# Fifth key block of the product with the values in two column tiles, and the 1e-9 of the softmax sums on ScalarE

## The chip, the cores and the metric

The kernel runs on one core of a Trainium2 chip. The metric is the device time of one execution in microseconds; of several runs the median is given. TensorE's granted clock is 2.4 GHz or 1.2 GHz, and the profile gives it as a share of the former.

## The reference

Attention with 2 batches, 8 heads, 576 positions and 64 channels per head, all in fp32, and behind it two MoE-like layers of 1152 tokens (512 to 2048 to 512 channels).

```python
scores = scale * np.matmul(q, k.transpose(0, 1, 3, 2))
...
scores = scores + bias.transpose(2, 0, 1)[None, :, :, :]
scores = scores - np.max(scores, axis=-1, keepdims=True)
attn = np.exp(scores)
attn = attn / (np.sum(attn, axis=-1, keepdims=True) + 1e-09)
return np.matmul(attn, v).astype(np.float32)
```

The bias comes from a small network over log-distances (hidden size 32); the two layers are `g(x @ w_in) @ w_out` with a rational function and a clipped square as g. The change touches the last three lines above: the 1e-9 and the product with v.

## The kernel before, in words

The queries are cut into blocks of 128 rows: a first one of 64 rows of both batches ("t") and four of 128 rows. A unit is a block with a pair of heads (`hp`), a pair is a unit with a batch: 4 pairs of the first kind and 32 full ones. For pair i and its heads e = 0 and 1 (tile t = 2i + e):

- `qk` (L322, TensorE): scores in PSUM, the two heads in two row tiles of the array;
- `ttr` (L337, VectorE): scores plus bias, with the row's minimum of the negated sum, into `P`;
- `exp` (L342, ScalarE): the exponential in place, with the row's sum into `m[:, 1, e]` (a second instruction reads the accumulator);
- `rec` (L346 and L347, VectorE, once for both heads): the sum plus 1e-9, and its reciprocal into `m[:, 2]`;
- `norm` (L146, mostly GpSimd): `P` times the reciprocal;
- `trans` (L367, TensorE) in three groups of three, each 128 by 128: of the 576 keys of both heads side by side nine blocks come out; block 4 holds the last 64 keys of head 0 and the first 64 of head 1 (whose keys run backwards);
- evacuation of each group to `PT` (L134, the helper `copy`, on ScalarE);
- `pv` (L380 and L383, TensorE): for block 4 one matmul of 128 columns with the values `Vt[hp][:, bb, 4]`, which hold zeros in the half of the rows that belongs to the other head; then for four blocks and both heads a matmul of 64 columns each into its half of the output's partitions;
- copies of the product (L400 ScalarE, L402 VectorE) into the inputs of the first layer, as a high and a low part.

All instructions of an engine run in the order in which they were written. A planner sets it: `at(step, engine, fn, pri, cost)` puts work into a step, `flex` leaves the engine to be chosen, and `run_step` goes through a step in order of `pri`, adds the costs to each engine's `load`, and for a `flex` takes the engine with the lowest load after its cost (`pick`); loads fall by a pace at each step. TensorE's work of a step comes behind the others', sorted likewise. For pair i the exponentials stand in steps 2i+2 and 2i+3, `rec` in 2i+4, the first group of transposes in 2i+6 and the others in 2i+7, their evacuations one step later, and `pv` in 2i+8. Between them lie the rows of the bias (L208, L206, L219, L142, L144) and the conversion of the layers' weights (L457 to L482).

`cst` is a tile of four columns of constants; three are in use (`setup2`), as bias operands of the layers' activations. Behind the attention the two layers run from a generator (`moe`, L652 and L695).

Of the kernel before, what the change touches and what calls it, by code (L numbers as in the profile page):

```python
# [8 lines left out]
AF = mybir.ActivationFunctionType  # L9
# [30 lines left out]
class Kernel:  # L40
# [21 lines left out]
    def setup2(self):  # L62
        nc, a, c = self.nc, self.a, self.const
        nc.gpsimd.memset(self.cst[:, 0:1], ADDC)
        nc.gpsimd.memset(self.cst[:, 1:2], 0.5)
        nc.gpsimd.memset(self.cst[:, 2:3], -0.5)

    def ab_consts(self):
        nc, c = self.nc, self.const
# [21 lines left out]
    def at(self, step, eng, fn, pri=0, cost=0.3):  # L91

        self.todo.setdefault(step, []).append((pri, eng, fn, cost))
# [191 lines left out]
    def attn(self, p, pq, ps, pss, x, cfg):  # L285
        nc, a, at = self.nc, self.a, self.at
        V, A, G, PE = nc.vector, nc.scalar, nc.gpsimd, nc.tensor
        halves = lambda z: z.rearrange("p (x c) -> p x c", x=2)
        K = [self.ring(f"K{h}").rearrange("p (b s) -> p b s", b=B) for h in range(H // 2)]
        Vt = [p.tile([128, B, 5, 128], F32, name=f"V{h}") for h in range(4)]  # L290
        self.K = K


        units = [(bk, hp) for bk in ("t", 0, 1, 2, 3) for hp in range(4)]
        pairs = []
        for n, (bk, hp) in enumerate(units):
            pairs += [(n, bk, hp, b) for b in ((0, 1) if bk != "t" else ("t",))]
        bias, Q, P, PT, sums, S_ = {}, {}, {}, {}, {}, {}
        vps = ps.tile([128, 2, 2, 128], F32, name="vps")
        first = {}  # L300
        for i, (n, *_) in enumerate(pairs):
            first.setdefault(n, 2 * i)

        def load_q(n):
            bk, hp = units[n]
            t = Q[n] = pq.tile([128, B, 128], F32, tag="Q", name="Q", bufs=4)
            if bk == "t":
                nc.sync.dma_start(t[:, :, 0:64], a["qt"][hp])
            else:
                nc.sync.dma_start(t, a["qm"][4 * bk + hp])  # L310

        def qk(i):

            n, bk, hp, b = pairs[i]
            for e in range(2):
                S_[2 * i + e] = pss.tile([128, 2, 512], F32, tag="s", name="sps", bufs=2)
            for x in range(2):
                for bb in (b,) if bk != "t" else range(2):
                    w, c = (128, 0) if bk != "t" else (64, 64 * bb)
                    for e in range(2):  # L320
                        r = slice(64 * e, 64 * e + 64)
                        PE.matmul(S_[2 * i + e][c:c + w, x, :288], lhsT=Q[n][r, bb, 0:w],  # L322
                                  rhs=f(K[hp])[r, bb, 288 * x:288 * x + 288], start=True, stop=True,
                                  tile_position=(64 * e, c))

        def tile_(t):
            i, e = divmod(t, 2)
            n, bk, hp, b = pairs[i]
            h = 2 * hp + e

            def ttr():
                if e == 0:
                    P[i] = p.tile([128, 2, S], F32, tag="P", name="P", bufs=cfg["pb"])
                    sums[i] = p.tile([128, 3, 2], F32, tag="m", name="m", bufs=6)
                o = P[i][:, 0] if e == 0 else P[i][:, 1][:, ::-1]
                bt = self.bias0[bk == 0][:, h] if bk in (0, "t") else bias[n, e][:]
                V.tensor_tensor_reduce(halves(o), S_.pop(t)[:, :, :288], halves(bt), -0.125, 3e38,  # L337
                                       ALU.add, ALU.min, sums[i][:, 0, e:e + 1])

            def exp():  # L340
                m, s = sums[i], P[i][:, e]
                A.activation(s, s, AF.Exp, bias=m[:, 0, e:e + 1], scale=-1.0, accum_out=m[:, 1, e:e + 1])  # L342

            def rec():
                m = sums[i]
                V.tensor_scalar(m[:, 2], m[:, 1], 1e-9, None, ALU.add)  # L346
                V.reciprocal(m[:, 2], m[:, 2])  # L347

            def norm(e_):
                s = P[i][:, e]  # L350
                self.copy(e_, s, s, sums[i][:, 2, e:e + 1])

            at(t + 1, "V", ttr, PAR["vp"][0], 0.69)
            at(t + 2, "A", exp, PAR["vp"][1], 0.77)
            if e:
                at(t + 2 + PAR["rec"], "V", rec, PAR["vp"][2])
            self.flex(2 * i + PAR['norm'] + PAR['norme'] * e, dict(G=PAR['cG'], V=PAR['cV'], A=PAR['cA']), norm, PAR['pe_'][0])

        def pair_(i):
            n, bk, hp, b = pairs[i]  # L360
            Pf = lambda: P[i].rearrange("p e c -> p (e c)")
            tp = {}

            def trans(c):
                t = tp[c] = ps.tile([128, 512], F32, tag="T", name="tps", bufs=3)
                for j in range(3):
                    PE.transpose(t[:, 128 * j:128 * j + 128], Pf()[:, 384 * c + 128 * j:384 * c + 128 * j + 128], self.ident)  # L367

            def evac(e, c):
                if c == 0:  # L370
                    PT[i] = p.tile([128, 9, 128], F32, tag="PT", name="PT", bufs=cfg["ptb"])
                dst = PT[i][:, 3 * c:3 * c + 3].rearrange("p a b -> p (a b)")
                self.copy(e, dst, tp.pop(c)[:, :384])

            def pv():
                o = vps[:, n % 2]
                for bb in ((b,) if b != "t" else (0, 1)):
                    c = slice(0, 128) if b != "t" else slice(64 * bb, 64 * bb + 64)
                    out = o[:, bb] if b != "t" else o[:, 0, c]
                    PE.matmul(out, lhsT=Vt[hp][:, bb, 4], rhs=PT[i][:, 4, c], start=True, stop=False)  # L380
                    for j in range(4):
                        for e in range(2):
                            PE.matmul(out[64 * e:64 * e + 64], lhsT=Vt[hp][:, bb, j, 64 * e:64 * e + 64],  # L383
                                      rhs=PT[i][:, (j, 5 + j)[e], c], start=False, stop=(j == 3))
                PT.pop(i), P.pop(i)

            for c in range(3):
                s = 2 * i + PAR['t0' if c == 0 else 't1']
                at(s, "P", lambda c=c: trans(c), PAR["pp"][2])
                self.flex(s + PAR['ev'], dict(A=PAR['eA'], V=PAR['eV']), lambda e, c=c: evac(e, c), PAR['pe_'][1])  # L390
            at(2 * i + PAR['pv'], "P", pv, PAR["pp"][3])
            if b != 0:
                o = {"t": [(0, 0, 128, 0)], 0: [(0, 0, 256, 128)], 1: [(1, 0, 256, 0)],
                     2: [(1, 0, 128, 256), (2, 128, 128, 0)], 3: [(2, 0, 256, 128)]}[bk]

                def out(k, u, c, w, d):
                    src = vps[:, n % 2].rearrange("p b q -> p (b q)")[:, c:c + w]
                    xh, xl = (x[k][u][:, hp, d:d + w] for k in range(2))
                    if k == 0:
                        A.activation(xh, src, AF.Copy)  # L400
                    else:
                        V.tensor_tensor(xl, src, f(xh), ALU.subtract)  # L402

                for y in o:
                    at(2 * i + PAR["xh"], "A", lambda y=y: out(0, *y), PAR["vp"][3])
                    at(2 * i + PAR["xl"], "V", lambda y=y: out(1, *y), PAR["vp"][4])

        def get_bias(n, e):
            bk, hp = units[n]
            h = 2 * hp + e  # L410
            bias[n, e] = self.load_bias(pq, bk, h, cfg["bias"])

        for t in range(2 * len(pairs)):
            tile_(t)
        for i in range(len(pairs)):
            at(2 * i, "P", lambda i=i: qk(i), PAR["pp"][0])
            pair_(i)
        for n in range(len(units)):
            at(first[n] - PAR["ql"], "end", lambda n=n: load_q(n), 1)
            for e in range(2) if n >= 8 else ():  # L420
                at(first[n] - cfg["ahead"] + e, "end", lambda n=n, e=e: get_bias(n, e), 2)
        for h in range(H):

            at(h, "G", lambda h=h: G.tensor_copy(self.bias0[0][64:128, h], self.bias0[0][0:64, h]), 0, 0.9)
            at(PAR['vl'][h], "end", lambda h=h: nc.sync.dma_start(Vt[h // 2][:, h % 2], a["v5"][h // 2, h % 2]), 3)

        return 2 * len(pairs) + 11
# [406 lines left out]
```

## Time and profile before

| what | value |
|---|---|
| time, median of 3 runs (lowest to highest) | 616.69 us (616.47 to 617.79) |
| profiled execution, span of its instructions | 615.9 us |
| difference of the two | 0.8 us |
| mean granted TensorE clock | 0.997 |
| busy: TensorE, VectorE, ScalarE, GpSimd | 95%, 78%, 66%, 57% |

The span runs from the first to the last instruction of one profiled execution; the time of a run holds what lies around it too. A busy share is that of the whole span, and the attention ends about a third into it, so what a change in the attention is worth is read from the windows and the chain of that part. The matmuls' ends are modelled and overlap: the starts tell more than the durations.

### The profile page before, as it was taken

The numbers are of one execution on the slowest core, as the hardware profiler recorded it, in microseconds if no ns is written. First come the engines' busy times: TensorE is split into PE (matmuls) and PEld (weight loads), VectorE is DVE, ScalarE is ACT, GpSimd is POOL, SyncE is SP. The second block draws the span as 40 slices with busy tenths as digits, with TensorE's granted clock in tenths as the row PEclk, the third lists the DMA queues.
The fourth block names the chain that finished last, engine by engine and source line by source line (L and its number), as shares of the span: only waits on it lengthen the run. The fifth ranks groups of instructions, "written<-read, shape, count | busy, mean of one in ns | idle before, by whom it ended". The sixth has DMA issues, their size and how long they took to land.

```text
span 615.9 us, 11246 instructions
## 1 busy us (share of the span) xinstructions
PE 584.2 (95%) x4084; PEld 519.1 (84%) x4084; DVE 479.0 (78%) x952; ACT 408.1 (66%) x878; POOL 348.7 (57%) x367
## 2 busy tenths in 40 slices
PE   5899998998999689999999999999999999999997
PEld 2356655566778589999999999999999999999997
DVE  6875777685679779889999888999996799594432
ACT  5976787776887799888878877644664554443330
POOL 0253334543557458679998886665674576384220
PEclk9999999999999999999999999999999999999999
DMA  6982256453644201232232221231323123020012
GB/s 207 252 273 80 83 180 205 139 185 104 190 154 150 92 24 46 69 102 70 69 103 69 70 69 51 88 102 69 103 103 103 57 85 99 1 70 1 24 42 89
DMA packets 25288, 62.71 MB, mean 102 GB/s; under 512 B 3601, under 2 KB 7569, under 8 KB 25233
## 3 DMA queue, kind: packets, MB, share of 16 engines
q1 hardware_dynamic: 25088, 61.90, 31.3%
q8 instruction: 32, 0.52, 0.4%
q14 instruction: 24, 0.19, 0.1%
q10 hardware_dynamic: 144, 0.10, 0.1%
HBM read 48.83 MB, written 9.62 MB: 95 GB/s over the span
## 4 chain that ended last, share of the span: by engine, by line
PE 79%; DVE 10%; ACT 5%; DMA 2%; issue 2%; POOL 1%; SPq 0%; DVEq 0%; POOLq 0%; ACTq 0%
PE outps L695 30%; PE inps L652 29%; PE sps L322 6%; PE vps L383 5%; PE bps L219 4%; PE tps L367 4%; PE vps L380 2%; DVE P L337 1%; DVE hid L208 1%; ACT PT L134 1%; DMA bias<-bd 1%; DVE wc L464 1%; ACT hid L206 1%; DVE wc L460 1%; DMA raw<-w 1%
## 5 line engine op out<-in xcount | busy, mean ns | idle before, releaser
L695 PE MATMUL outps<-gh,wo 128*128 128x384 f32 x768 | 209.7, 335 | 0.0
L558 POOL TENSOR_TENSOR gl<-v,gh 128x384 fp32r<-128x384 f32 x96 | 110.4, 1150 | 79.3 <-ACT gh L554 74.8
L695 PEld LDWEIGHTS outps<-gh,wo 128*128 128x128 f32 x768 | 139.9, 188 | 0.0
L695 PE MATMUL outps<-gl,wo 128*128 128x384 f32 x384 | 128.4, 334 | 0.0
L652 PE MATMUL inps<-x,wh 128*128 128x384 f32 x384 | 99.8, 341 | 5.5 <-DVE x L402 3.8
L146 POOL TENSOR_SCALAR P<-P,m 128x576 f32<-128x576 f32 x72 | 56.6, 792 | 68.8 <-DVE m L347 51.4
L337 DVE CUSTOM_DVE_ANT_0 P<-sps,bias 128x576 f32<-128x576 f32 x72 | 54.0, 750 | 35.4 <-PE sps L322 20.8
L652 PEld LDWEIGHTS inps<-x,wh 128*128 128x128 f32 x384 | 70.2, 190 | 6.7 <-DVE x L402 4.1
L695 PEld LDWEIGHTS outps<-gl,wo 128*128 128x128 f32 x384 | 72.1, 188 | 0.0
L521 ACT ACTIVATE v<-inps,cst 128x384 f32<-128x384 f32 x48 | 27.8, 580 | 66.7 <-PE inps L652 63.8
L652 PE MATMUL inps<-x2l,wh 128*128 128x384 f32 x192 | 64.7, 337 | 1.7 <-DVE x2l L628 1.7
L545 DVE SCALAR_TENSOR_TENSOR v<-v 128x384 f32<-128x384 f32 x48 | 39.5, 823 | 34.1 <-ACT v L521 33.9
L652 PE MATMUL inps<-x,wl 128*128 128x384 f32 x192 | 65.1, 339 | 0.0
L652 PE MATMUL inps<-x2h,wh 128*128 128x384 f32 x192 | 64.7, 337 | 0.0
L652 PE MATMUL inps<-x2h,wl 128*128 128x384 f32 x192 | 64.6, 336 | 0.0
L134 ACT ACTIVATE PT<-tps 128x384 f32<-128x384 f32 x108 | 48.6, 488 | 23.3 <-PE tps L367 23.0
L554 ACT ACTIVATE gh<-v 128x384 fp32r<-128x384 f32 x96 | 50.6, 527 | 20.1 <-DVE v L546 18.9
L525 POOL TENSOR_TENSOR q<-h,q 128x384 f32<-128x384 f32 x48 | 48.7, 1015 | 26.3 <-ACT q L518 25.8
L342 ACT ACTIVATE P<-P,m 128x576 f32<-128x576 f32 x72 | 55.9, 776 | 11.3 <-DVE m L337 11.3
L464 DVE SCALAR_TENSOR_TENSOR wc<-raw,wc 128x512 int32<-128x512 int32 x64 | 59.9, 946 | 0.0
L367 PEld LDWEIGHTS tps<-late,P 128*128 128x128 f32 x324 | 34.6, 141 | 20.8 <-issue 14.5
L219 PE MATMUL bps<-hid,w2s 128*32 128x288 f32 (+17 forms) x416 | 41.6, 472 | 8.4 <-DVE hid L208 7.0
(79 smaller groups left out, 1192.1 us busy)
## 6 DMA issues: line engine op xcount, KB each, us to landing
raw<-w SPq DMA_DIRECT2D x64, 512.0 KB
bd<-bbuf SPq DMA_DIRECT2D x24, 295.5 KB
bias<-bd SPq DMA_DIRECT2D x24, 288.0 KB
bias<-bbuf SPq DMA_DIRECT2D x12, 288.0 KB
V<-v SPq DMA_DIRECT2D x8, 320.0 KB
K<-kc SPq DMA_DIRECT2D x4, 576.0 KB
out<-acc SPq DMA_DIRECT2D x12, 192.0 KB
Q<-qm SPq DMA_DIRECT2D x16, 128.0 KB
```

The source lines that it names most:

```text
L134: nc.scalar.activation(out, x, AF.Copy, scale=scale)
L146: nc.gpsimd.tensor_scalar(out, x, scale, 1.0, ALU.mult, ALU.mult)
L219: nc.tensor.matmul(st[x][32 * j:32 * j + 32, :w], lhsT=w2, rhs=hid[j][:, x * w:x * w + w], start=True, stop=True, tile_position=(0, 32 * j))
L337: V.tensor_tensor_reduce(halves(o), S_.pop(t)[:, :, :288], halves(bt), -0.125, 3e38, ALU.add, ALU.min, sums[i][:, 0, e:e + 1])
L342: A.activation(s, s, AF.Exp, bias=m[:, 0, e:e + 1], scale=-1.0, accum_out=m[:, 1, e:e + 1])
L367: PE.transpose(t[:, 128 * j:128 * j + 128], Pf()[:, 384 * c + 128 * j:384 * c + 128 * j + 128], self.ident)
L464: return [(dict(V=0.7), lambda e: V.scalar_tensor_tensor(tc, words[:, :, 0], 29, tc, ALU.logical_shift_right, ALU.bitwise_or))]
L525: return [lambda: G.tensor_tensor(o["q"], o["h2"], o["q"], ALU.add)] if m == 0 else []
L554: return [lambda: A.activation(gh, o["v"], AF.Copy)]
L558: return [lambda: G.tensor_tensor(gl, o["v"], f(o["gh"]), ALU.subtract)]
L652: nc.tensor.matmul(ps[:, :U], lhsT=w[:, c], rhs=y[:, c], start=(t == 0), stop=(t == 11))
L695: nc.tensor.matmul(ps[:, :U], lhsT=w[:, c], rhs=y, start=(t == 0), stop=(t == 11))
```

## The change

The product with the fifth key block (block 4) is written as two matmuls of 64 columns, one for each head, into the two halves of the output's partitions, like the other four blocks; it stays first and now carries the start of the sum. The addition of 1e-9 leaves VectorE; an activation with identity on ScalarE, with the constant as bias operand, stands behind the second exponential of a pair (same step, next in `pri`) and has a planner's cost of 0.1. The constant takes the fourth column of `cst`.

```diff
         nc.gpsimd.memset(self.cst[:, 2:3], -0.5)
+        nc.gpsimd.memset(self.cst[:, 3:4], 1e-9)
...
+            def eps():
+                m = sums[i]
+                A.activation(m[:, 2], m[:, 1], AF.Identity, bias=self.cst[:, 3:4])
+
             def rec():
                 m = sums[i]
-                V.tensor_scalar(m[:, 2], m[:, 1], 1e-9, None, ALU.add)
                 V.reciprocal(m[:, 2], m[:, 2])
...
             if e:
+                at(t + 2, "A", eps, PAR["vp"][1] + 0.1, 0.1)
                 at(t + 2 + PAR["rec"], "V", rec, PAR["vp"][2])
...
-                    PE.matmul(out, lhsT=Vt[hp][:, bb, 4], rhs=PT[i][:, 4, c], start=True, stop=False)
-                    for j in range(4):
+                    for j in (4, 0, 1, 2, 3):
                         for e in range(2):
                             PE.matmul(out[64 * e:64 * e + 64], lhsT=Vt[hp][:, bb, j, 64 * e:64 * e + 64],
-                                      rhs=PT[i][:, (j, 5 + j)[e], c], start=False, stop=(j == 3))
+                                      rhs=PT[i][:, (j, 5 + j if j < 4 else 4)[e], c],
+                                      start=(j == 4), stop=(j == 3))
```

## Rows read from the trace of the kernel before

**Rows 1.** The page, busy us (share of the span) and instructions of each engine.
```profile
PE 584.2 (95%) x4084; PEld 519.1 (84%) x4084; DVE 479.0 (78%) x952; ACT 408.1 (66%) x878; POOL 348.7 (57%) x367
```

**Rows 2.** The page, chain that ended last, share of the span by line.
```profile
PE outps L695 30%; PE inps L652 29%; PE sps L322 6%; PE vps L383 5%; PE bps L219 4%; PE tps L367 4%; PE vps L380 2%; DVE P L337 1%; DVE hid L208 1%; ACT PT L134 1%; DMA bias<-bd 1%; DVE wc L464 1%; ACT hid L206 1%; DVE wc L460 1%; DMA raw<-w 1%
```

**Rows 3.** Windows: us, length, busy us of each engine, PEclk, DMA share, GB/s.
```profile
20.00:190.00 170.00, 157.69 (x1560) 104.05 (x1562) 121.94 (x355) 131.25 (x320) 77.69 (x113) 1.00 0.53 164
200.00:220.00 20.00, 14.40 (x83) 13.47 (x83) 14.02 (x26) 14.28 (x30) 7.76 (x8) 0.91 0.22 74
```

**Rows 4.** Waits, 0 to 213 us: waiter <- releaser, us in total, times, longest.
```profile
ACT PT L134 <- PE tps L367: 23.0, 25, 2.0
DVE P L337 <- PE sps L322: 20.8, 17, 2.6
...
PEld vps L380 <- ACT PT L134: 12.0, 21, 2.1
```

**Rows 5.** Timeline of TensorE, a product at 181 us: start, us, instructions.
```profile
180.27 1.20 PE L367 MATMUL tps<-late,P 128*128 128x128 f32 x9
181.40 0.49 PE L380 MATMUL vps<-PT,V 128*128 128x128 f32 x2
181.81 1.09 PE L383 MATMUL vps<-PT,V 128*64 128x128 f32 x16
182.84 0.51 PE L322 MATMUL sps<-K,Q 64*128 64x288 f32 x1
```

**Rows 6.** Timeline of TensorE, a product at 150 us.
```profile
149.86 0.39 PE L380 MATMUL vps<-PT,V 128*128 128x128 f32 x2
150.18 1.09 PE L383 MATMUL vps<-PT,V 128*64 128x128 f32 x16
151.21 0.51 PE L322 MATMUL sps<-K,Q 64*128 64x288 f32 x2
```

**Rows 7.** Timeline of TensorE, the product of the first pair.
```profile
37.82 0.33 PE L380 MATMUL vps<-PT,V 128*128 128x64 f32 x2
38.08 0.69 PE L383 MATMUL vps<-PT,V 128*64 128x64 f32 x16
38.70 0.44 PE L380 MATMUL vps<-PT,V 128*128 128x64 f32 x2
39.06 0.69 PE L383 MATMUL vps<-PT,V 128*64 128x64 f32 x16
39.68 0.52 PE L322 MATMUL sps<-K,Q 64*128 64x288 f32 x2
```

**Rows 8.** Groups by line and form, and line L82: busy us, mean ns; duration.
```profile
L134 ACT ACTIVATE PT<-tps 128x384 f32<-128x384 f32 x108 | 48.6, 488 | 23.3 <-PE tps L367 23.0
...
L383 PE MATMUL vps<-PT,V 128*64 128x128 f32 x512 | 35.0, 279 | 0.0
...
L383 PE MATMUL vps<-PT,V 128*64 128x64 f32 x128 | 5.5, 228 | 0.0
...
L521 ACT ACTIVATE v<-inps,cst 128x384 f32<-128x384 f32 x48 | 27.8, 580 | 66.7 <-PE inps L652 63.8 <-POOL wo L149 2.7
...
L346 DVE TENSOR_SCALAR m<-m 128x2 f32<-128x2 f32 x36 | 8.2, 227 | 0.0
...
L82 ACT ACTIVATE rt<-rt x1: 203/203/203, 95.0 to 95.0; 128x1 f32<-128x1 f32 x1
```

**Rows 9.** Chain that ended last in order of time: start, us, what.
```profile
190.35 0.51 DVE m L346
```

**Rows 10.** Timeline of ScalarE, 164 to 169 us.
```profile
164.01 0.19 ACT L342 ACTIVATION_READ_ACCUMULATOR P<-P,m 128x1 f32 x1
...
165.09 0.87 ACT L134 ACTIVATE PT<-tps 128x384 f32<-128x384 f32 x2
...
168.84 0.87 ACT L134 ACTIVATE PT<-tps 128x384 f32<-128x384 f32 x2 [0.98 <-PE tps L367]
```

**Rows 11.** Timeline of VectorE, the removed addition behind that exponential.
```profile
165.20 0.16 DVE L346 TENSOR_SCALAR m<-m 128x2 f32<-128x2 f32 x1
```

## The prediction

> **What bounds the kernel now.** I read the busy table first: TensorE is busy for 95% of the span and no other engine for over 78% [rows 1]. Of the chain that ended last TensorE's lines hold 80%, the layers' two groups 59% of it; those of the product with the values (L383 5%, L380 2%) hold 7% of 615.9 us, some 43 us [rows 2]. The part that the change touches is 20 to 190 us, by the windows: TensorE 158 of 170 us, ScalarE 131, VectorE 122 at full clock [rows 3]; the MoE layers behind it repeat a matmul group back to back and contain nothing of the change. The waits say who follows whom: ScalarE's evacuations of the transposes waited 23.0 us for TensorE, VectorE's score pass 20.8 us for TensorE, and TensorE 12.0 us for those evacuations ahead of the product [rows 4]. So TensorE's order is the backbone, with a short loop through ScalarE (transposes, evacuation, product).
>
> **TensorE: the fifth block.** An fp32 matmul is two passes in the trace (a weight load and a matmul each): two for the fifth block, 16 for the other eight, in two column tiles. In [rows 5] the two full passes start at 181.40 and the column tiles at 181.81, which is 0.41 us for one key block of five; the 16 passes and the turn to the next form take 181.81 to 182.84, 1.03 us for four blocks. A pass lasts 0.28 us in the mean [rows 8], so the 16 starts lie within 1.09 - 0.28 = 0.81 us: were each alone at the full form's 0.11 us (nine transposes start within 1.20 - 0.28 us), they would take 1.7. The two column tiles therefore run side by side, one pair of passes in 0.81/7, some 0.115 us. After the change the block is two such pairs, 0.23 us, so the product lasts 1.03 + 0.23 = 1.26 us instead of 1.44: **0.18 us less**.
>
> That holds where the product starts when its data comes, for then the turn from the transposes to column tiles is over by the time that the data is there. It is the pattern of [rows 5] (the product 0.1 us or more later than the transposes allow) in 24 of the 32 full products. In the other 8 it follows the transposes at once: 149.86 to 151.21, 1.35 us, where the full passes cost 0.32 us, of which some 0.10 us is the turn (0.32 less two passes of 0.11). There the turn now comes ahead of the product: 1.26 + 0.10 = 1.36, a gain of 0 [rows 6]. The Trainium skill, TensorEngine Tiling (Array Packing), Key Properties, says that a change of tiling mode drains TensorE. By that rule the turn stands ahead of all 32 products and costs its 0.10 us in each, so the 24 would gain 0.08 us instead of 0.18 and the sum below would be 3.1 us instead of 5.0; the 8 products agree with it, for the 24 no row of before shows it.
>
> The four products of the first 64 rows (both batches in one) turn four times now: 37.82, 38.08, 38.70, 39.06 and out at 39.68, 1.86 us [rows 7]. A pass of 64 columns lasts 0.23 us [rows 8], a pair of them takes (0.69 - 0.23)/7 = 0.066 us, so afterwards it is 19 intervals of 0.066, a turn in of 0.10 and 0.16 out (39.68 less the last start, 39.06 + 0.69 - 0.23): 1.51 us. That is 0.35 us less for each, and 0.45 if the turn in lies in a wait; I take 0.4.
>
> How much lies on the path: following the chain through the products, it runs along TensorE through all four of the first kind and through 19 of the 24; it is elsewhere near 93 to 104 us (three products) and from 197 us on (two). Sum: 19 x 0.18 + 4 x 0.4 = **5.0 us**; from both sides 0 (another engine late instead) and 24 x 0.18 + 4 x 0.45 = 6.1.
>
> **VectorE loses an instruction** of 0.16 us (0.23 in the mean) ahead of each reciprocal, 36 in all [rows 8], 8 us of its 122. Most of it lies in waits. On the chain it stands in three places only, the largest at 190.35 with 0.51 us [rows 9]; with two of about 0.2 I take **0.8 us**, between 0 and 8.
>
> **ScalarE gains one.** Nearest rows: 0.203 us for one element, and 92 ns between an evacuation without a pointer operand and a layer activation with one (488 and 580 ns, both 384 elements) [rows 8]. So 0.20 to 0.30 us each, and since it reads what the exponential's accumulator read has just written, it cannot start under that read's last 0.1 us. I take 0.25 us in ScalarE's queue, 36 x 0.25 = 9 us. The Trainium skill (ScalarE: Activation LUTs, What ACT_TABLE_LOAD costs) gives about 0.28 us for an activation with a pointer bias and few elements; by it the sum would be 10 us, and no run here shows this form.
>
> Behind it in the queue come the copy of the product, a conversion, and the evacuation that the next product waits for. Cover: ScalarE waited at least 0.34 us for the transposes ahead of that evacuation in 25 of 36 pairs, as 0.98 at 168.84; there it costs nothing. In 11 the wait was below 0.13, as at 165.09, where the evacuations follow the exponential and two others without a gap [rows 10]. In five of these the product waits for the evacuation and a new instruction stands ahead of it; one is off the chain. So 4 x 0.25 = **1.0 us** on the path, and at most 9.
>
> The reciprocal now waits for this instruction, and behind it on VectorE the next score pass and the copies that release TensorE. The smallest distance from the exponential's read (ends 164.20) to the removed addition (165.20) is 1.0 us [rows 10, 11], against 0.25: no new wait. The fourth memset runs on GpSimd beside three like it, long before any pair: 0.
>
> The planner adds 0.1 to ScalarE's load 36 times. Working its sums through with the table of costs, 44 of 808 choices change engine, all by step 49, and ScalarE has two fewer in total. I take 0, with 0.5 us either way.
>
> **Sum.** -5.0 - 0.8 + 1.0 = -4.8 us on the span of 615.9. The path of before is not the only one: ScalarE has 38.75 of 170 us idle [rows 3], 1.8 in the 8 us of two products, and gets 0.5 more work in a shorter time; and behind 190 us VectorE and ScalarE stand on the chain. I give a fifth back: **-3.9 us**. The time shown, 616.69, lies 0.8 us above the span; the same difference gives **612.8 us**.
>
> **Rivals.**
> A, *ScalarE takes over* (slower). Its queue becomes the loop's bound: every evacuation ahead of a product comes 0.25 us later and TensorE's gain turns into waiting. It decides once ScalarE's idle time ahead of the evacuation is below 0.25 us in most pairs instead of 11. Price: 36 x 0.25 = 9 us, in half of the pairs still under a wait, less the 0.8 of VectorE: 616.69 + 4.5 - 0.8 = 620.4. For it: the conversions from 150 us on leave ScalarE hardly a gap [rows 10]. Against: the 23.0 us it waits for TensorE.
> B, *absorbed*. The products get shorter, but the handover to the MoE (weights, VectorE's queue, which the window from 200 us shows with TensorE at 14.4 of 20 us and a mean granted clock of 0.91, a stretch at 1.2 GHz [rows 3]) starts no earlier: 616.69 less about 0.8 = 615.9. That stretch can also come out up to 1.8 us longer or shorter (0.09 x 20).
> C, *the tiles of the fifth block don't overlap*: the change doesn't do what it says. Four passes of 0.11 instead of two pairs: 0.22 us more each, the gain of 0.18 is gone, 36 x 0.04 + 1.0 - 0.8 = 1.6 more: 618.3. Against: the same form overlaps in all 36 products now.
>
> **Chances.** Forecast 0.67 (own range 609.8 to 614.9: no giveback and the clock's 1.8 at one end, half of the gain lost at the other); A 0.12; B 0.17; C 0.04. I give 609.8 to 617.2. Within 0.2% is 615.46 to 617.92, about what a measurement of this kernel can tell from no change. Faster takes the forecast and a part of B, 0.72; same the rest of B and a part of A and C, 0.16; slower 0.12.
>
> **What would show it.** Right: the full-form passes of L380 are gone and the column passes are ten pairs in a product instead of eight; the product from first pass to the next form takes some 1.26 us; L383's share of the chain falls; the distance between products from 153 to 190 us shrinks by about 0.15 us each. ScalarE's new instruction lasts 0.2 to 0.3 us, and its waits for the transposes stay above 15 us in total. Wrong: waits of the product for the evacuation grow from 12 us to 18 or more (A); the products shorten and the first MoE matmul group after the last product starts where it did (B); single passes at 0.11 us (C).

## The result, and the profile after

| | before | after |
|---|---|---|
| time, median of 4 executions each (lowest to highest) | 617.24 us (616.47 to 618.34) | 610.07 us (609.56 to 612.08) |
| ratio, 95% interval | | 0.9893 [0.9871, 0.9916] |
| span of the profiled execution | 615.9 us | 607.7 us |

The change makes the kernel 7.2 us faster by the medians; 610.07 lies 2.7 us under the 612.8 forecast and inside the range. The changed kernel was run again later beside a kernel before at 616.86: 611.02, ratio 0.9905 [0.9886, 0.9924]; its nine executions together have a median of 610.40. A ratio here is not the quotient of the two medians (that would be 0.9884); the two ways differ by up to 0.001 in what follows, 0.6 us, and the intervals reach about 1 us to either side, so sizes taken from medians are no surer than that.

The page after, busy us (share of the span) and instructions of each engine, then the chain by line:

```profile
PE 576.9 (95%) x4164; PEld 513.6 (85%) x4164; DVE 473.9 (78%) x918; ACT 415.9 (68%) x912; POOL 351.7 (58%) x368
...
PE outps L700 30%; PE inps L657 29%; PE vps L387 6%; PE sps L323 5%; PE bps L220 4%; PE tps L372 4%; DMA bias<-bd 2%; ACT PT L135 1%; ACT hid L207 1%; DVE hid L209 1%; DVE P L338 1%; DVE wc L465 1%; DVE wc L469 1%; DMA raw<-w 1%; ACT bbuf L135 1%
```

Against [rows 1], TensorE has 80 more passes and is busy for 7.3 us less; VectorE has 34 instructions fewer, ScalarE 34 more. Of the chain the product has 6% (L387) where L383 and L380 had 7%, and bias loads (DMA) rose from 1% to 2% [rows 2].

Waits after, 0 to 213 us (waiter <- releaser, us in total, times, longest):

```profile
DVE P L338 <- PE sps L323: 18.7, 18, 2.7
...
PEld vps L387 <- ACT PT L135: 14.7, 21, 2.3
...
ACT PT L135 <- PE tps L372: 12.9, 21, 1.5
```

ScalarE's wait for the transposes fell from 23.0 to 12.9 us, TensorE's wait for the evacuations grew from 12.0 to 14.7 [rows 4]; a second profile of the same program has 13.2 and 12.3. The loop through ScalarE became tighter without taking over.

TensorE's timeline after: a product whose data comes late, one that follows the transposes at once, and the first pair's (start, us, instructions):

```profile
174.83 1.04 PE L372 MATMUL tps<-late,P 128*128 128x128 f32 x8
175.97 1.31 PE L387 MATMUL vps<-PT,V 128*64 128x128 f32 x20
177.21 0.51 PE L323 MATMUL sps<-K,Q 64*128 64x288 f32 x2
...
143.80 0.55 PE L372 MATMUL tps<-late,P 128*128 128x128 f32 x3
144.28 1.31 PE L387 MATMUL vps<-PT,V 128*64 128x128 f32 x20
145.52 0.51 PE L323 MATMUL sps<-K,Q 64*128 64x288 f32 x2
...
36.79 1.39 PE L387 MATMUL vps<-PT,V 128*64 128x64 f32 x40
38.11 0.51 PE L323 MATMUL sps<-K,Q 64*128 64x288 f32 x2
```

From the product's first pass to the next form: 1.24 us in both full ones, where it was 1.44 and 1.35 [rows 5, 6], and 1.32 us in the first, where it was 1.86 [rows 7]. The full passes are gone; twenty column passes (ten pairs) stand in their place, forty in the first kind.

Where the time went, by the starts of the products on TensorE's timeline (us; change against before in brackets; one profiled execution each):

| kernel | start to 1st product | 1st to 5th | 5th to 34th | 34th to the end |
|---|---|---|---|---|
| before | 37.82 | 21.05 | 135.30 | 421.69 |
| after | 36.79 (-1.02) | 18.99 (-2.06) | 132.11 (-3.19) | 419.83 (-1.86) |
| after, again | 37.30 (-0.52) | 18.99 (-2.06) | 131.44 (-3.86) | 421.45 (-0.24) |
| tiles alone | 37.95 (+0.13) | 19.04 (-2.01) | 132.94 (-2.36) | 421.75 (+0.06) |
| addition's move alone | 37.25 (-0.57) | 21.05 (0) | 134.60 (-0.70) | 421.82 (+0.12) |
| tiles, no addition | 37.15 (-0.67) | 18.99 (-2.06) | 131.62 (-3.69) | 421.95 (+0.25) |

The second profile of the same program shows what the columns can tell: 1st to 5th repeats exactly, the start is off by 0.5, 5th to 34th by 0.7, and the last by 1.6 for a reason that is no part of the change (last section).

### The profile page after: what moved, and what is told of

It reads as the page before. It is cut to its first block, busy times and chain, and to the rows that moved or that the text cites. A ratio compares the mean times of both kernels' runs of the same rounds, so it can differ in the third digit from the quotient of the medians.

```text
span 607.7 us, 11380 instructions
## 1 busy us (share of the span) xinstructions
PE 576.9 (95%) x4164; PEld 513.6 (85%) x4164; DVE 473.9 (78%) x918; ACT 415.9 (68%) x912; POOL 351.7 (58%) x368
## 4 chain that ended last, share of the span: by engine, by line
PE 78%; DVE 8%; ACT 6%; DMA 4%; issue 2%; POOL 1%; SPq 0%; DVEq 0%; ACTq 0%; POOLq 0%
PE outps L700 30%; PE inps L657 29%; PE vps L387 6%; PE sps L323 5%; PE bps L220 4%; PE tps L372 4%; DMA bias<-bd 2%; ACT PT L135 1%; ACT hid L207 1%; DVE hid L209 1%; DVE P L338 1%; DVE wc L465 1%; DVE wc L469 1%; DMA raw<-w 1%; ACT bbuf L135 1%
## 5 line engine op out<-in xcount | busy, mean ns | idle before, releaser
L147 POOL TENSOR_SCALAR P<-P,m 128x576 f32<-128x576 f32 x72 | 58.6, 821 | 64.2 <-DVE m L351 59.7
L387 PE MATMUL vps<-PT,V 128*64 128x128 f32 (+1 forms) x800 | 47.7, 267 | 13.0 <-ACT PT L135 5.1
L135 ACT ACTIVATE PT<-tps 128x384 f32<-128x384 f32 x108 | 48.8, 487 | 13.0 <-PE tps L372 12.9
L387 PEld LDWEIGHTS vps<-PT,V 128*64 128x64 f32 x800 | 39.7, 137 | 19.9 <-ACT PT L135 14.7
```

The costliest lines, as they stand in the source:

```text
L135: nc.scalar.activation(out, x, AF.Copy, scale=scale)
L147: nc.gpsimd.tensor_scalar(out, x, scale, 1.0, ALU.mult, ALU.mult)
```

## The experiments

Times are medians of 5 to 12 executions, beside the kernel before on the same chip (617.19, 616.86 or 616.71 us). The kernels without the 1e-9 leave out only that.

**The parts one by one.** Tiles alone keeps VectorE's addition; the move alone keeps the full-form matmul of block 4; the third is the kernel before with the planner's 0.1 and no instruction.

```diff
 # tiles alone, against the changed kernel
+                V.tensor_scalar(m[:, 2], m[:, 1], 1e-9, None, ALU.add)
-                at(t + 2, "A", eps, PAR["vp"][1] + 0.1, 0.1)
 # cost alone, against before
+                at(t + 2, "A", lambda: None, PAR["vp"][1] + 0.1, 0.1)
```

> The fifth block in two column tiles, all else as before (addition on VectorE, no planner's cost). Theory 1, TensorE's products set the time: the products take 1.24 to 1.31 us as in the changed kernel (1.34 to 1.44 and 1.86 before), and most of the gain is here: 4 x 0.55 + 19 x 0.18 = 5.6 us, 611 to 612 us. Theory 2, the gain comes from the addition's move and the planner's other choices: 614 us or more, though the products are as short. Theory 3, a good part is where the stretch at 1.2 GHz falls: the attention part gains 5 to 6 us at 190 us, but the first long group of the layers takes about 3.7 us where the stretch falls on it and 2.4 where not.

> The addition on ScalarE with its planner's cost, the fifth block in full form as before. Theory 1: VectorE's relief of 0.8 us and ScalarE's 1.0 us on the path cancel: 616 to 618 us. Theory 2: 613 to 615 us. If ScalarE took over (rival A of the prediction): 619 us or more.

> The kernel before with 0.1 added to ScalarE's load in the planner at the 36 places and no instruction added or moved: 44 choices between ScalarE and VectorE change. Theory 1: within 0.5 us of the kernel before. Theory 2: 1.5 us or more faster.

Measured: tiles alone 613.68 us, ratio 0.9953 [0.9937, 0.9968]; the move alone 615.74, 0.9975 [0.9961, 0.9988]; the cost alone 617.44, 1.0005 [0.9993, 1.0017]. So by the medians the tiles are worth 3.5 us (by the ratio 2.9, interval 2.0 to 3.9), the move 1.5, the planner's other choices nothing. The two parts make 5.0 us; together they gave 6.3 to 6.8 (median of nine against the three values of before).

**No addition at all**, on either engine (leaves the 1e-9 out):

```diff
-                V.tensor_scalar(m[:, 2], m[:, 1], 1e-9, None, ALU.add)
-                V.reciprocal(m[:, 2], m[:, 2])
+                V.reciprocal(m[:, 2], m[:, 1])
```

> The column tiles, and the addition of 1e-9 left out altogether (a row's sum holds the exponential of its maximum, 1, so the sum is at least 1 and the addition does not change it in fp32). No new instruction on ScalarE, none on VectorE, no planner's cost. Theory 1: the changed kernel's time less what the new instruction costs on the path, 1.0 us: about 609 us; idle time of ScalarE ahead of the evacuations back to 18 us or more. If the new instruction is hidden everywhere: 610 us, as the changed kernel. Theory 2 (planner's choices matter): 612 us or more, since they are those of before.

Measured: 610.58 us, 0.9898 [0.9878, 0.9918], 3.1 us under the tiles alone. Part of this may lie in the granted clock: nine of ten executions of the tiles alone had a mean of 0.993 or 0.994, three of the six here 0.997. Those at 0.993 and 0.994 alone have medians of 613.85 and 611.07, 2.8 us apart; the two profiled spans (611.7 and 609.7, both at 0.994) 2.0. Whether the clock differs by chance or comes with the kernel is not shown. Taking VectorE's addition away is worth 2 to 3 us, not 0.8.

**The price on ScalarE.** The changed kernel again; without the new instruction but with its planner's cost; with the instruction issued twice.

```diff
 # without (1e-9 left out)
-                at(t + 2, "A", eps, PAR["vp"][1] + 0.1, 0.1)
+                at(t + 2, "A", lambda: None, PAR["vp"][1] + 0.1, 0.1)
 # twice
                 A.activation(m[:, 2], m[:, 1], AF.Identity, bias=self.cst[:, 3:4])
+                A.activation(m[:, 2], m[:, 1], AF.Identity, bias=self.cst[:, 3:4])
```

> The changed kernel unaltered, for more of its executions beside the others. Theory 1 (the products' shortening and VectorE's relief add up, -4.4 and -0.7 us by the distance between the first and the 34th product): the product of the last full-attention step again 5 to 5.5 us earlier relative to the first product. Theory 3 (the place of the stretch at 1.2 GHz): executions with a mean clock of 0.997 lie 1 to 2 us below those with 0.993; the median of all lies at 610 to 611 us.

> The changed kernel with the planner's cost kept, so that every choice of engine is that of the changed kernel, but without the new instruction on ScalarE: the addition of 1e-9 is left out. What remains against the changed kernel is the instruction's price alone. Theory 1 (1.0 us on the path): 609.0 us. If it is hidden (as the version with neither addition nor planner's cost, 610.6 us, suggests): within 0.4 us of the changed kernel.

> The changed kernel with its new activation issued twice (the same values written again): 36 more instructions of 0.29 us on ScalarE, at some 0.2 us each in its queue. If ScalarE has room: under 0.5 us slower than the changed kernel. If ScalarE is at its bound from 160 us on, as the evacuations there that no longer wait suggest: 1.5 to 3 us slower. Rival A of the prediction at full price: 7 us slower.

Measured: again 611.02 us, 0.9905 [0.9886, 0.9924]; without 610.95, 0.9907 [0.9889, 0.9925]; twice 612.92, 0.9940 [0.9920, 0.9960]. The first copy costs nothing that can be told from zero, the second 1.9 us. The waits of ScalarE's evacuation for the transposes, one row from each kernel, say why. Without:

```profile
ACT PT L134 <- PE tps L367: 21.5, 30, 1.8
```

Twice (once: 12.9, above):

```profile
ACT PT L135 <- PE tps L373: 6.6, 14, 1.1
```

The first copy was paid out of 21.5 us of waiting. With the second, the total is 6.6 us, and the 5th to the 34th product take 133.76 us, where they took 131.19 without the instruction and 132.11 and 131.44 with one.

**The two kinds of product.** Tiles only in the four first products, and only in the 32 full ones (the addition on VectorE in both):

```diff
+                    T = b == "t"    # or b != "t"
+                    if not T:
+                        PE.matmul(out, lhsT=Vt[hp][:, bb, 4], rhs=PT[i][:, 4, c], start=True, stop=False)
-                    for j in (4, 0, 1, 2, 3):
+                    for j in (4, 0, 1, 2, 3) if T else range(4):
```

> The kernel before with the fifth block in column tiles only in the four products of the first 64 rows (addition on VectorE, no planner's cost). Theory 1: 4 x 0.55 = 2.2 us at the fifth product, and 2.0 us in the time: 615.2 us. If what the first products gain is absorbed by the bias rows' loads at 90 to 104 us: within 0.5 us of the kernel before. By the prediction's 0.4 us for each: 615.6.

> The fifth block in column tiles only in the 32 full products, full form in the four of the first 64 rows (addition on VectorE, no planner's cost). Theory 1: from the fifth to the 34th product 2.4 us less, as with the tiles everywhere (the prediction had 19 x 0.18 = 3.4), and 2 us in the time: 615 us. If the two groups do not add up (all tiles 613.7, first ones alone 615.7): 616 us or more.

Measured: the first four 615.67 us, 0.9971 [0.9955, 0.9987], 1.2 us (interval 0.8 to 2.8); the full ones 614.21, 0.9958 [0.9942, 0.9975], 2.5 us (1.5 to 3.6). They add up to 3.7, the tiles' 3.5 within the noise. The first ones' gain at the fifth product is 2.01 us, of which 0.67 is given back by the 34th; the full ones take 3.20 us off the stretch between.

**What the addition cost on VectorE.** The longest removed additions in the trace before, GpSimd's timeline and VectorE's at 181 us:

```profile
181.04 1.28 POOL L149 TENSOR_TENSOR wo<-wc,wo 128x512 fp32r<-128x512 f32 x1
...
181.09 1.26 DVE L346 TENSOR_SCALAR m<-m 128x2 f32<-128x2 f32 x1
182.38 0.17 DVE L347 RECIPROCAL m<-m 128x2 f32<-128x2 f32 x1
```

An addition over two elements lasts 1.26 us and ends within 0.03 us of the GpSimd instruction that began just before it; the reciprocal of the same two elements, right behind it, takes 0.17. The others that are long do the same: 0.33 at 33.44, 0.88 at 161.49, and [rows 9]'s at 190.27 (0.58, ending 190.85; GpSimd's L144 ends at 190.82). The Trainium skill (SBUF — State Buffer, SBUF: two separate sides) gives a mechanism: VectorE in a two-port mode and GpSimd take a shared port pair as an exclusive lock for a whole instruction, and whoever comes second blocks until it ends. The rows agree; the mode itself is in no row. One addition is an exception: begun at 193.69, 0.49 us into a GpSimd instruction (L146, 1.18 us there, where the same line took 0.74 at 180.34), it took 0.16 us. To tell holding from the instruction's own time, the addition was replaced by a reduction over one element, which copies the sum (1e-9 left out) and stands in the same place:

```diff
-                V.tensor_scalar(m[:, 2], m[:, 1], 1e-9, None, ALU.add)
+                V.tensor_reduce(m[:, 2], m[:, 1].rearrange("p (e o) -> p e o", o=1), mybir.AxisListType.X, ALU.add)
```

> All products in column tiles, and in the addition's place on VectorE a reduction over one element, which copies the sum (the 1e-9 is left out): an instruction of VectorE at the same place, not in the form that lasted 0.4 to 1.1 us where it began beside a GpSimd instruction and ended with it. Theory 1a, the price of the addition is the holding by GpSimd: none of the 36 lasts over 0.25 us, and the time is 611.5 us or less, near the version without any (610.6). Theory 1b, it is the 0.2 us of an instruction at each place, on the path some eight times: 613 us or more, near the version with the addition (613.7).

Measured: 612.33 us, 0.9933 [0.9916, 0.9951], between the two expectations. The instruction's group (duration ns min/median/max, first and last start) with the tiles alone:

```profile
L346 DVE TENSOR_SCALAR m<-m x36: 149/158/1087, 29.5 to 189.4; 128x2 f32<-128x2 f32 x36
```

And as a reduction, with a moment from GpSimd's timeline and from VectorE's:

```profile
L346 DVE TENSOR_REDUCE m<-m x36: 139/146/151, 29.2 to 188.6; 128x2 f32<-128x2 f32 x36
...
156.51 1.27 POOL L149 TENSOR_TENSOR wl<-wc,wh 128x512 fp32r<-128x512 f32 x1
...
156.74 0.14 DVE L346 TENSOR_REDUCE m<-m 128x2 f32<-128x2 f32 x1
156.92 0.17 DVE L347 RECIPROCAL m<-m 128x2 f32<-128x2 f32 x1
```

The reduction runs through GpSimd's instruction in 0.14 us; with the tiles alone the addition at 157.11, begun 0.22 us into the same kind of instruction (156.89, 1.28 us), lasted 1.09. All four additions held with the tiles alone (at 33.48, 157.11, 176.74 and 186.02, for 0.33, 1.09, 0.41 and 0.57 us) have such a counterpart: the reductions at 33.17, 156.74, 176.49 and 185.66 begin inside the same GpSimd instructions and take 0.14 to 0.15. So the hold is shown to depend on VectorE's kind of instruction. In time, 613.68 to 612.33, 1.35 us, goes to the holds (1.5 among executions at 0.993 and 0.994); 612.33 to 610.58, 1.75 us, to a plain instruction of 0.15 us in the way 36 times (1.3 at equal clock). How the two divide is sure to about 1 us only: the two kernels ran on different chips, and by their ratios, whose intervals overlap, the holds are 1.2 us.

**The planner's cost in the changed kernel**, set to 0:

```diff
-                at(t + 2, "A", eps, PAR["vp"][1] + 0.1, 0.1)
+                at(t + 2, "A", eps, PAR["vp"][1] + 0.1, 0.0)
```

> The changed kernel with the planner's cost of the new instruction 0 instead of 0.1: the choices of engine are those of the kernel before. Theory 1: the choices are worth nothing, within 0.5 us of the changed kernel (610.4 us over both its groups of executions). If they make room for the new instruction: 1 us or more slower.

Measured: 610.43 us, 0.9896 [0.9878, 0.9914], no different from the changed kernel. No kernel of these is clearly faster than it.

## Why the prediction was right, and where it was not

**The length of a product: right.** 1.24 us against 1.26 forecast. The turn also: eight products that follow the transposes at once pay it ahead (their first pass starts 0.20 us after the last transpose's, 0.11 before), so 0.11 + 1.35 became 0.20 + 1.24 and nothing is gained. Those that wait for data start no later after their data, and gain 0.17 to 0.20. The Trainium skill's rule that a mode change drains TensorE (TensorEngine Tiling (Array Packing), Key Properties) shows only where no wait hides it; its sum of 3.1 us instead of 5.0 rested on all 32 paying. The 3.5 us measured for the tiles alone lie nearer to 3.1, but not for that reason, since the products that wait did gain 0.17 to 0.20. Rival C is out.

**The first products: mis-sized, low.** 1.32 us, where I had 1.51 (or 1.41 with the turn in a wait): 0.54 less for each instead of 0.4. Three of the four pay 0.09 of it ahead (their first pass, too, starts 0.20 instead of 0.11 us after the last transpose's), and 2.06 us are left at the fifth product. In single passes of the trace the first pair after the turn takes 0.11 us and each pair behind it 0.058; I had spread the first pair's time over all (0.066), and put the turn in, 0.10, inside the product, where it lies ahead of it.

**How much lies on the path: mis-sized, high.** 5.0 us forecast, 3.5 measured alone. The first ones brought 1.2 of their 1.6 and the full ones 2.5 of 3.4; neither term is outside its own interval, but 5.0 is outside that of the tiles (2.0 to 3.9). What is missing is missing late in the attention. In the profile of the tiles alone the lead over before (how much earlier a product starts) grows from 1.88 us at the fifth product to 4.39 at the 26th, and is 4.24 at the 34th, though each of the eight products between is 0.17 to 0.20 us shorter. The sign that I had named for this stretch, distances between products from 153 to 190 us shorter by about 0.15 us each, failed: the nine from the 24th to the 33rd product shrank by 0.17 us in all with the tiles alone, and by 0.23 and 0.91 in the two profiles of the changed kernel, instead of 1.35. There, a product shortened by 0.2 us isn't followed by everything else 0.2 us earlier. This is the fifth given back, found in the tiles' term.

What holds the rest back there is open, and these are single profiles: from the 26th to the 34th product the kernel with tiles only in the full products gains 0.70 us, and the one with tiles only in the first four, which changes nothing in this stretch, loses 1.29. In the first profile of the changed kernel the lead falls from 6.42 us at the 27th product to 5.42 at the 31st, where VectorE's score pass waits for bias loads. Waits, after:

```profile
DVE P L338 <- DMA bias<-bd: 5.0, 4, 2.4
```

Before (the same wait):

```profile
DVE P L337 <- DMA bias<-bd: 1.0, 2, 0.7
```

The loads do not explain it: the lead is back at 6.28 by the 34th product, and in the second profile, where this wait is 0.2 us in all, it falls as well (6.35 at the 29th, 5.34 at the 30th, 6.43 at the 34th).

**VectorE's relief: mis-sized, and the step that failed.** I took 0.8 us, from the places where the chain of before stood on the addition; without it the kernel with tiles is 2 to 3 us faster. The chain names one path; an instruction ahead of every reciprocal, and so of the next score pass and of GpSimd's norm, is near many. And I took "0.16 us, 0.23 in the mean" as two sizes of one thing [rows 8], where the gap between them meant a few additions held for up to 1.26 us, the one at 190.35 [rows 9] among them.

**ScalarE's price: mis-sized, high.** 1.0 us forecast, 0.07 measured (611.02 less 610.95, five executions each, inside the noise; the nine executions with the instruction have 610.40, less than the five without). The duration was near, 0.29 against 0.25:

```profile
157.30 0.20 ACT L343 ACTIVATION_READ_ACCUMULATOR P<-P,m 128x1 f32 x1
157.54 0.29 ACT L347 ACTIVATE m<-m,cst 128x2 f32<-128x2 f32 x1
157.74 0.43 ACT L405 ACTIVATE x<-vps 128x128 fp32r<-128x128 f32 x2
```

This is ScalarE's timeline after; the instruction starts 0.24 us after the accumulator's read did, and the next one 0.20 us later. The four products at 0.25 us on the path cannot be seen: that ScalarE waits 12.9 us, not the "above 15" named as the sign, shows that the cover was used and not exceeded. Rival A had the right mechanism and the wrong point: with two copies it begins.

**The planner: right**, nothing (both ways).

**The sum.** Forecast -5.0 - 0.8 + 1.0 + 0.9 = -3.9; measured -3.5 (tiles, their giveback within) - 3.1 + 0.1 = -6.5, against -6.3 to -6.8. Of the 2.6 us between the two sums the addition is 2.3 and ScalarE 0.9; the path goes the other way with 0.6 (5.0 less the 0.9 given back, against 3.5). With the equal-clock 2.0 to 2.8 for the addition the measured sum is -5.4 to -6.2: part of what the changed kernel shows is then unexplained interaction or chance.

That the time fell inside the range is partly luck. The tiles brought less than forecast, and the terms for VectorE and ScalarE, which were off by 2.3 and 0.9 us, carried the time to the low end. That end, 609.8, was reached only with the clock's 1.8 us, and its own terms make 610.1 (616.69 - 4.8 - 1.8), beside which 610.07 stands.

Rival B, that the handover absorbs the gain, is out: tiles alone lead by 4.2 us at the 34th product (2.01 + 2.36 less 0.13 at the start) and by 4.2 in the span (611.7 against 615.9).

One number of the working was wrong: span and time differ by 1.8 us in one execution (609.56 and 607.7), not 0.8; the 616.69 is the median and belongs to another execution than the span of 615.9.

## What to carry to other kernels

Price a tiny instruction by its longest occurrences and by what runs beside them: where mean and median differ, look up the longest in the timeline, and if they end with an instruction of another engine, moving the small one can be worth more than its own time. Here a 64-column block among column tiles was cheaper as two tiles than as one full-form matmul (1.24 us a product instead of 1.34 to 1.44), and the turn between forms cost nothing where the data came late anyway; what a shorter product is worth has still to be read stretch by stretch. An engine with slack hides a small addition until its waits are nearly used up; a run that issues it twice tells how near that is.

## What the runs showed that was not expected

Two profiles of the changed program differ by 1.5 us in span (607.7 and 609.2). It lies in where a stretch at half the clock falls near the handover to the layers. Windows (us, length, busy us of each engine, PEclk, DMA share, GB/s), before:

```profile
212.00:217.00 5.00, 3.89 (x14) 3.89 (x15) 3.96 (x9) 1.74 (x5) 1.72 (x2) 0.66 0.02 5
```

After:

```profile
198.00:202.00 4.00, 4.00 (x20) 3.67 (x15) 3.07 (x5) 3.59 (x8) 2.01 (x2) 0.57 0.00 0
204.00:210.00 6.00, 3.96 (x23) 3.68 (x22) 5.17 (x11) 4.86 (x11) 3.75 (x5) 1.00 0.12 46
```

After, again:

```profile
198.00:202.00 4.00, 4.00 (x24) 4.00 (x24) 3.52 (x5) 3.97 (x9) 1.95 (x2) 1.00 0.00 0
206.00:210.00 4.00, 3.69 (x12) 3.69 (x13) 3.16 (x7) 0.96 (x3) 1.01 (x1) 0.57 0.01 4
```

A mean granted clock of 0.57 is mostly the 1.2 GHz level. TensorE's timeline of the first layer's second group (start, us, instructions, idle before), after:

```profile
206.32 0.62 PE L657 MATMUL inps<-x,wh 128*128 128x384 f32 x2 [2.04 <-DVE x L407]
206.78 0.35 PE L657 MATMUL inps<-x,wl 128*128 128x384 f32 x1
206.97 0.52 PE L657 MATMUL inps<-x,wh 128*128 128x384 f32 x2
```

After, again:

```profile
206.31 0.93 PE L657 MATMUL inps<-x,wh 128*128 128x384 f32 x2 [3.99 <-DVE x L407]
207.04 0.52 PE L657 MATMUL inps<-x,wl 128*128 128x384 f32 x1
207.36 0.84 PE L657 MATMUL inps<-x,wh 128*128 128x384 f32 x2
```

In the first profile the lower clock falls on the group ahead, behind which TensorE waits for VectorE's copy of the product anyway: the wait is 2.04 us instead of 3.99, and the second group starts at the same time (206.32 and 206.31), at full clock. In the second profile, as before the change (213.11, 3.74 us for the twelve matmuls), it falls on the second group, on the chain, which takes 3.93 instead of 2.39 us. So 1.5 us between the first two profiled spans is where the clock fell, in the same program (what they differ by ahead of it, 0.5 one way and 0.7 the other, nearly cancels); ahead of the drop TensorE had idled, 1.98 us before the product at 197.03 in the one and 3.99 us before the second group in the other. The medians hold both cases, and the prediction had allowed 1.8 us for it.
